# Low words of the experts' second matrices and of their token blocks, made by adding transfers in place of VectorE subtractions

## The chip, the cores and the metric

The kernel runs on one core of one Trainium2 chip. The metric is the device time of one execution in microseconds; what is compared is the median over several executions. All inputs and outputs are float32.

## The reference

Three stages follow each other: an attention with a feature map, a feed-forward layer (FFN), and a mixture of experts (MoE).

```python
def _attn_ref(q, k, v, w_phi):               # 4 batches, 8 heads, 576 tokens, 64 wide
    ...
    num = np.einsum('bhsf,bhfd->bhsd', q_p, kv)
    den = np.einsum('bhsf,bhf->bhs', q_p, z)[..., None] + 1e-06
    return (num / den).astype(np.float32)

def _moe_ref(x, U, V, w_ch1, w_ch2):         # FFN: 512 -> 2048 -> 512
    ...
    u = x + h.transpose(0, 2, 1)
    ch = np.maximum(u @ w_ch1, 0.0) @ w_ch2
    return (u + ch).astype(np.float32)

def _moe2_ref(x, w_gate, w_local, w1, w2):   # 8 experts, each 512 -> 1024 -> 512
    ...
            h = np.maximum(x[b, s] @ w1[e], 0.0)
            out[b, s] = p[e] * (h @ w2[e])
    return out.astype(np.float32)
```

## The kernel before

**Two words for each number.** TensorE multiplies float32r, a float32 with fewer bits. To keep float32 accuracy each matrix stands in two words: the high word is the value rounded to float32r, the low word what is left, rounded again. A product is three matmuls: high by high, high by low, low by high (`three`, L1168 to L1170, and `mm2`, L1494 to L1496). So a tile of weights `w` holds [high, low] of 128 x 512, and a tile of tokens `x` holds [high, low] of two 128-row blocks, 288 tokens wide in the MoE (384 in the FFN).

**Who makes the words.** `w_end` makes a weight tile: ScalarE (ACT) casts the float32 buffer to the high word (L379), then the low word is buffer minus high word, on VectorE (DVE) or GpSimd (POOL) as `either` picks; in the late part it picks VectorE (`both`, L373). `x_end` does the same for token tiles: the cast at L651, the subtraction through `paused` (L76).

```python
nc.scalar.copy(out=w[:, 0], in_=f[:, :512])
eng = yield from either(eng, 512, f, w)
both(eng, w[:, 1], f, f32(w[:, 0]), ALU.subtract)
```

**The MoE stage.** For each of the 4 batches the expert that most tokens chose is computed for the whole batch, in two units of half of its hidden width each; the other experts' tokens are handled by a loop at the end. A unit has four pieces of the first matrix, named A (seven sums of them for batches 1 to 3, where a seven-product scheme is used), and four pieces of the second matrix, named V (`VS`). The token blocks of the MoE have the key "m": 4 tiles for batch 0 and 7 for each other batch. Weights come from HBM by SyncE's (SP's) queue into `raw` and `row` buffers (L604, L608). When a low word is made, its source buffer goes back to a free list, and the next load may take it. There are 14 weight tiles, 9 token tiles and 8 `row` buffers.

**What sets the order.** The program is written out by a planner in Python, before anything runs. TensorE's order is a list of products, gone through step by step; after each step `side` lets side jobs (generators) put instructions onto the other engines. `gate` and `either` hold a job back until the planner's own clock for the engine and the buffers (`free`, `touched`) says that it would start no later than TensorE's clock plus a slack. All engines then run their instructions in that fixed order, joined by semaphores.

**The router.** `route(b)` chooses the expert of a batch, in stages that `PLANS` spreads over the steps: gate matmuls (L1551), two ACT copies of their result into a `row` buffer (L1552), transposes of it (L1558), small VectorE operations, transposes back (L1605), ACT copies into three `row` buffers (L1609), a scan, a reduction and a product on VectorE (L1612, L1616, L1619), and two small transfers on POOL's queue (L1623 `mine`, L1624 `sall`). It waits with its stages while no `row` buffer is free. POOL's queue also carries the FFN's token loads (L756).

Of the kernel before, what the change touches and what calls it, by code (L numbers as in the profile page):

```python
# [8 lines left out]
F32R = mybir.dt.float32r  # L9
# [3 lines left out]
ALU = mybir.AluOpType  # L13
# [30 lines left out]
def model(ctx, tc, kq, vx, wphi, ident, up, vp, wff, wg, wmoe1, wmoe2, rconst, outT):  # L44
    nc = tc.nc
# [12 lines left out]
    def f32(ap):  # L58
        return ap.bitcast(F32)
# [14 lines left out]
    def paused(eng, **kw):  # L74

        eng.tensor_tensor(**kw)  # L76
        if eng is nc.gpsimd and pauses[0] and free["POOL"] >= landed[0]:
            nc.gpsimd.drain()

    def in_halves(eng, dst, a, b, n, op):  # L80

        for sl in (slice(0, n // 2), slice(n // 2, n)):
            paused(eng, out=dst[:, sl], in0=a[:, sl], in1=b[:, sl], op=op)
# [82 lines left out]
    late = {}  # L166
# [3 lines left out]
    free = {"PE": 0.0, "DVE": 0.0, "ACT": 0.0, "POOL": 0.0}  # L170
    port = [0.0]
    touched = {}
# [13 lines left out]
    def cost(eng, n):  # L186
        return {"DVE": 0.085 + n / 960, "ACT": 0.17 + n / 1330, "POOL": 0.05 + n / 340}[eng]
# [4 lines left out]
    def book(eng, dur, *keys):  # L192

        at = max([free[eng]] + [touched.get(id(k), 0.0) for k in keys])
        free[eng] = at + dur
        for k in keys:
            touched[id(k)] = free[eng] + SYNC
        return free[eng]

    def gate(eng, dur, *keys):  # L200

        if not late:
            yield "step"
        while late and not force[0]:
            at = max([free[eng], port[0] if eng == "DVE" else 0.0] + [touched.get(id(k), 0.0) for k in keys])
            if at + (0.0 if eng == "POOL" else dur) <= free["PE"] + SLACK[eng][at_step[0]]:
                break
            yield "wait"
        emitted[0] += 1
        force[0] = False  # L210
        if late:
            if eng == "DVE":
                free[eng] = max(free[eng], port[0])
            at = book(eng, dur, *keys)
            if eng == "DVE":
                port[0] = at

    def either(eng, n, *keys):

        if not late:  # L220
            yield "step"
            emitted[0] += 1
            return eng
        while True:
            best = None
            for e, name, bias in ((nc.gpsimd, "POOL", 0.0), (nc.vector, "DVE", BIAS)):
                dur = cost(name, n)
                at = max([free[name], port[0]] + [touched.get(id(k), 0.0) for k in keys])
                ok = (name == "DVE" or not lean[0]) and at + (0.0 if name == "POOL" else dur) <= free["PE"] + SLACK[name][at_step[0]]
                if (ok or force[0] and (name == "DVE" or not lean[0])) and (best is None or at + dur + bias < best[0]):  # L230
                    best = (at + dur + bias, e, name, dur)
            if best is not None:
                break
            yield "wait"
        emitted[0] += 1
        force[0] = False
        free[best[2]] = max(free[best[2]], port[0])
        port[0] = book(best[2], best[3], *keys)
        return best[1]

    def transfer(kb, at=None):

        wire[0] = max(free["PE"] if at is None else at, wire[0]) + kb / 400
        return wire[0] + 2.5
# [46 lines left out]
    def later(on, issue):  # L291

        if late:
            waiting.append((touched.get(id(on), 0.0), issue))
        else:
            issue()
# [8 lines left out]
    def take(free_):  # L305

        while not free_:
            yield "blocked"
        return free_.pop(0)

    BLOCKS = ("A11", "A12", "A21", "A22")
    VS = ("V1", "V0", "V3", "V2")
# [55 lines left out]
    def both(eng, out, a, b, op):  # L368
        out, a, b = out[:, :512], a[:, :512], b[:, :512]
        if eng is nc.gpsimd:  # L370
            in_halves(eng, out, a, b, 512, op)
        else:
            eng.tensor_tensor(out=out, in0=a, in1=b, op=op)  # L373

    def w_end(u, s, f, eng, back=None):

        w = u.w[s] = yield from take(wfree)
        yield from gate("ACT", cost("ACT", 512), f, w)
        nc.scalar.copy(out=w[:, 0], in_=f[:, :512])  # L379
        eng = yield from either(eng, 512, f, w)  # L380
        both(eng, w[:, 1], f, f32(w[:, 0]), ALU.subtract)
        u.done.add(s)
        if back is not None:
            back.append(f)
# [83 lines left out]
    def w_more():  # L468
# [9 lines left out]
        def end(s, f, back=None):  # L478
            spawn("w", 2, w_end(u, s, f, nc.gpsimd, back))
# [25 lines left out]
    def w_seven(u, get, free_, eng, p, due, flat=False, pre=""):  # L505

        def end(s, f, back=None):
            spawn("w", due + (flat and s[0] == "S"), w_end(u, pre + s, f, eng, back))
# [49 lines left out]
    def w_ffn(u, due):  # L558

        def get(name):  # L560
            while (u, name) not in pieces:
                yield "blocked"
            return pieces.pop((u, name))

        spawn("w", due, fetch(u, ZSEVEN if u.g in ZU else SEVEN) if u.g > 1 else parked(u, SEVEN))
        yield from w_seven(u, get, rows, nc.gpsimd, nc.gpsimd, due)
        if u.g in ZU:
            yield from w_seven(u, lambda s: get(ZV[s]), rows, nc.gpsimd, nc.gpsimd, due, pre="z")
            return
        for s in VS:  # L570
            f = yield from get(s)
            spawn("w", due, w_end(u, s, f, nc.gpsimd, rows))
# [65 lines left out]
    def spot(key, s):  # L638
# [2 lines left out]
        w = CH if key[0] == "m" else TW  # L641
        return slice(2 * k, 2 * k + 2), slice((2 * key[1] + t) * w, (2 * key[1] + t + 1) * w)

    def x_end(key, s, r, keep, own=None, then=None):

        x = xo.setdefault(key, {})[s] = yield from take(xfree)
        wanted[1] -= then is not None and key[0] == "f"
        n_ = CH if key[0] == "m" else TW
        keys = (x,) if own is None else (x, own)
        yield from gate("ACT", cost("ACT", 2 * n_), *keys)  # L650
        nc.scalar.copy(out=x[:, 0, :, :n_], in_=r)  # L651
        for k in (slice(0, 2),) if late else (slice(0, 1), slice(1, 2)):
            use = yield from either(nc.gpsimd, n_ * (k.stop - k.start), *keys)
            paused(use, out=x[:, 1, k, :n_], in0=r[:, k], in1=f32(x[:, 0, k, :n_]), op=ALU.subtract)
        if keep:
            def send():
                nc.sync.dma_start(out=f32(xd[key[1]][XD.index(s)]), in_=f32(x))
                if late:
                    transfer(768)
            later(x, send)  # L660
        xdone.add((key, s))
        if then is not None:
            then()
# [4 lines left out]
    def x_plain(key, names):  # L668

        for s in names:  # L670
            k, t = spot(key, s)
            yield from x_end(key, s, y[:, k, t], key[0] == "p" and s != "B12")

    def x_sums(key, due):
# [18 lines left out]
        def end(s, r, then=None):  # L693
            spawn("x", due, x_end(key, s, as_x(r), True, r, (lambda: rows.append(r)) if then is None else then))
# [16 lines left out]
    def x_diff(key, due):  # L711
# [11 lines left out]
        def end(s, r, then=None):  # L723
            spawn("x", due, x_end(key, s, as_x(r)[:, :, :w], keep, r, (lambda: rows.append(r)) if then is None else then))
# [1220 lines left out]
```

## Time and profile before

| what | value |
|---|---|
| median of 3 executions | 759.97 us (759.38 to 762.55) |
| the profiled execution | 760.08 us |
| its span, first to last instruction | 758.2 us |
| PE, PEld, DVE, ACT, POOL busy | 745.3, 724.1, 637.7, 351.7, 72.5 us |
| granted TensorE clock | 1.0 |
| bytes moved by DMA | 124.27 MB |

PE is TensorE's matmuls and PEld its weight loads, which overlap them. Matmuls are pipelined, so one matmul's duration is longer than the distance to the next. Some records of matmuls can be missing. Issuing a DMA is not counted as busy on SP and ACT; the time to landing is listed apart. The trace's line numbers are those of the kernel before; in the changed kernel the same lines stand 12 or 25 further down.

### The profile page before, as it was taken

The page shows a single profiled execution, that of the slowest core. Times are in us where ns is not written, and L with a number is a line of the kernel's source. Part 1 is how long each engine was busy: PE and PEld are TensorE (multiplying, and loading weights), DVE is VectorE, ACT ScalarE, POOL GpSimd, SP SyncE. Part 2 cuts the span into 40 slices and gives each one's busy share as a digit, 9 for nine tenths or more (in the row PEclk, how much of TensorE's full clock was granted, in tenths as well). Part 3 has the DMA queues.
Part 4 walks back from the last instruction along what each step waited for, and adds up shares of the span by engine and source line. Part 5 has one row for each costly group of instructions (what it writes and reads, how often), then busy time and mean ns, then how long its engine had stood idle before and what let it go on. Part 6 is the DMA issues. An engine that isn't in the chain of part 4 may idle for free. (4 is left out here: it accounts for less than half of the span.)

```text
span 758.2 us, 18724 instructions
## 1 busy us (share of the span) xinstructions
PE 745.3 (98%) x7656; PEld 724.1 (96%) x7656; DVE 637.7 (84%) x1277; ACT 351.7 (46%) x769; POOL 72.5 (10%) x116
## 2 busy tenths in 40 slices
PE   7999999999999999999999999999999999999997
PEld 5899898999999999999999999999999999999997
DVE  6889899777569999999799485879877899999975
ACT  5677777665152343313223133343545455555450
POOL 0212233111110000100101001010000000000000
PEclk9999999999999999999999999999999999999999
DMA  6444755324468897950469004482363144243421
GB/s 203 151 132 126 260 183 189 111 80 154 181 242 328 302 332 284 346 171 29 166 241 339 18 1 157 153 287 84 114 210 101 32 125 143 68 136 108 136 69 65
DMA packets 52728, 124.27 MB, mean 164 GB/s; under 512 B 5472, under 2 KB 29152, under 8 KB 52640
## 3 DMA queue, kind: packets, MB, share of 16 engines
q1 hardware_dynamic: 43024, 87.20, 34.1%
q0 software_dynamic: 6160, 32.39, 12.3%
q10 hardware_dynamic: 3456, 3.46, 1.3%
q8 instruction: 61, 1.00, 0.5%
q14 instruction: 27, 0.22, 0.1%
HBM read 88.81 MB, written 34.23 MB: 162 GB/s over the span
## 5 line engine op out<-in xcount | busy, mean ns | idle before, releaser
L1169 PE MATMUL psf<-x,w 128*128 128x384 f32 (+1 forms) x576 | 184.1, 320 | 0.6 <-POOL x L76 0.6
L1168 PE MATMUL psf<-x,w 128*128 128x384 f32 (+1 forms) x576 | 184.4, 320 | 0.0
L1170 PE MATMUL psf<-x,w 128*128 128x384 f32 (+1 forms) x576 | 183.9, 319 | 0.0
L1494 PE MATMUL psf<-h,w 128*128 128x384 f32 (+1 forms) x576 | 182.8, 317 | 0.0
L1495 PE MATMUL psf<-h,w 128*128 128x384 f32 (+1 forms) x576 | 182.3, 316 | 0.0
L1496 PE MATMUL psf<-h,w 128*128 128x384 f32 (+1 forms) x576 | 182.2, 316 | 0.0
L1146 ACT ACTIVATE h<-psf 128x384 fp32r<-128x384 f32 (+1 forms) x144 | 62.9, 457 | 106.7 <-DVE psf L1129 77.7
L1168 PEld LDWEIGHTS psf<-x,w 128*128 128x128 f32 x576 | 108.3, 188 | 1.4 <-issue 1.4
L1169 PEld LDWEIGHTS psf<-x,w 128*128 128x128 f32 x576 | 108.2, 188 | 1.0 <-POOL x L76 0.9
L1494 PEld LDWEIGHTS psf<-h,w 128*128 128x128 f32 x576 | 108.1, 188 | 0.5 <-issue 0.5
L1170 PEld LDWEIGHTS psf<-x,w 128*128 128x128 f32 x576 | 108.2, 188 | 0.0
L1495 PEld LDWEIGHTS psf<-h,w 128*128 128x128 f32 x576 | 108.1, 188 | 0.0
L1496 PEld LDWEIGHTS psf<-h,w 128*128 128x128 f32 x576 | 108.1, 188 | 0.0
L1129 DVE TENSOR_TENSOR y<-psf,y 128x384 f32<-128x384 f32 (+1 forms) x132 | 69.1, 530 | 24.9 <-PE psf L1496 21.3
L1131 DVE SCALAR_TENSOR_TENSOR h<-psf,h 128x384 fp32r<-128x384 f32 (+1 forms) x148 | 69.0, 508 | 21.5 <-ACT h L1146 20.9
L379 ACT CAST w<-row 128x512 fp32r<-128x512 f32 x79 | 46.7, 620 | 53.9 <-DVE row L373 31.8
L373 DVE TENSOR_TENSOR w<-row,w 128x512 fp32r<-128x512 f32 x79 | 52.9, 687 | 10.6 <-ACT w L379 10.6
L857 DVE TENSOR_REDUCE mx<-pj 128x6 f32<-128x768 f32 (+2 forms) x49 | 45.8, 935 | 6.8 <-PE pj L854 6.7
L858 DVE TENSOR_TENSOR pg<-pj,mx 128x768 f32<-128x768 f32 (+2 forms) x49 | 46.1, 941 | 2.5
L887 PE MATMUL kv<-vt,ek 128*64 128x65 f32 (+1 forms) x1152 | 47.1, 230 | 0.8 <-DMA vt<-in_vx 0.8
L756 POOL DMA_DIRECT2D x<-xd x41 | 22.0, 535 | 269.4 <-PE psf L1170 232.5
L1129 DVE TENSOR_TENSOR u<-psf,p 128x384 f32<-128x384 f32 (+1 forms) x64 | 32.4, 513 | 15.3 <-PE psf L1170 14.2
(136 smaller groups left out, 1126.7 us busy)
## 6 DMA issues: line engine op xcount, KB each, us to landing
x<-xd POOLq DMA_DIRECT2D x41, 768.0 KB, 6.9
raw<-in_wff SPq DMA_DIRECT2D x32, 512.0 KB, 3.6
xd<-x SPq DMA_DIRECT2D x21, 768.0 KB, 4.9
raw<-in_wmoe SPq DMA_DIRECT2D x35, 256.0 KB, 3.4
kq<-in_kq SPq DMA_DIRECT2D x14, 576.0 KB, 4.5
row<-in_wmoe SPq DMA_DIRECT2D x29, 256.0 KB, 4.0
vt<-in_vx SPq DMA_DIRECT2D x16, 325.0 KB, 3.0
ud<-y SPq DMA_DIRECT2D x4, 1152.0 KB, 6.6
```

Source lines behind the costliest of these rows:

```text
L373: eng.tensor_tensor(out=out, in0=a, in1=b, op=op)
L379: nc.scalar.copy(out=w[:, 0], in_=f[:, :512])
L887: nc.tensor.matmul(out[c], lhsT=e[:, half, i, c], rhs=rhs, start=(tl == 0 and half == 0), stop=(tl == 8 and half == 1), skip_group_check=True)
L1129: nc.vector.tensor_tensor(**kw)
L1131: nc.vector.scalar_tensor_tensor(op1=op1, **kw)
L1146: hat[t, f] = act(lambda: nc.scalar.activation(out=hhi, in_=src, func=ACTF.Relu), n_, ready)
L1168: nc.tensor.matmul(ps, lhsT=w[:, 0, c], rhs=x[:, 0, k, :n_], start=(first and k == 0), stop=False, skip_group_check=True)
L1169: nc.tensor.matmul(ps, lhsT=w[:, 0, c], rhs=x[:, 1, k, :n_], start=False, stop=False, skip_group_check=True)
L1170: nc.tensor.matmul(ps, lhsT=w[:, 1, c], rhs=x[:, 0, k, :n_], start=False, stop=(stop and k == 1), skip_group_check=True)
L1494: nc.tensor.matmul(ps, lhsT=wh, rhs=hhi, start=(k == 0), stop=False)
L1495: nc.tensor.matmul(ps, lhsT=wl, rhs=hhi, start=False, stop=False)
L1496: nc.tensor.matmul(ps, lhsT=wh, rhs=hlo, start=False, stop=(k == 3))
```

## The change

For the V pieces of the experts' matrices (`added`) and for all token tiles of the MoE, in the late part of the program, the subtraction on VectorE or GpSimd is replaced by two steps: ACT writes the negated high word into the low word's place, and a DMA on POOL's queue adds the float32 value onto it. The source buffer is booked as busy until the larger of the planner's estimate of the transfer and `ADD_LAT`, 4.0, after the issue.

```diff
+    ADD_LAT = 4.0
+
+    def added(u, s):
+        return u.kind=="moe" and s in VS
+
     def w_end(u, s, f, eng, back=None):
 
         w = u.w[s] = yield from take(wfree)
         yield from gate("ACT", cost("ACT", 512), f, w)
         nc.scalar.copy(out=w[:, 0], in_=f[:, :512])
-        eng = yield from either(eng, 512, f, w)
-        both(eng, w[:, 1], f, f32(w[:, 0]), ALU.subtract)
+        if late and added(u, s):
+            yield from gate("ACT", cost("ACT", 512), f, w)
+            nc.scalar.mul(out=w[:, 1], in_=f32(w[:, 0]), mul=-1.0)
+            yield from gate("POOL", 0.6, f, w)
+            nc.gpsimd.dma_start(out=w[:, 1], in_=f.bitcast(F32R)[:, :512], accum_op=ALU.add)
+            touched[id(w)] = touched[id(f)] = max(transfer(512, free["POOL"]), free["POOL"] + ADD_LAT)
+        else:
+            eng = yield from either(eng, 512, f, w)
+            both(eng, w[:, 1], f, f32(w[:, 0]), ALU.subtract)
...
+    def x_low(x, r, keys, n_):
+
+        for k in (slice(0, 2),) if late else (slice(0, 1), slice(1, 2)):
+            use = yield from either(nc.gpsimd, n_ * (k.stop - k.start), *keys)
+            paused(use, out=x[:, 1, k, :n_], in0=r[:, k], in1=f32(x[:, 0, k, :n_]), op=ALU.subtract)
...
         nc.scalar.copy(out=x[:, 0, :, :n_], in_=r)
-        for k in (slice(0, 2),) if late else (slice(0, 1), slice(1, 2)):
-            use = yield from either(nc.gpsimd, n_ * (k.stop - k.start), *keys)
-            paused(use, out=x[:, 1, k, :n_], in0=r[:, k], in1=f32(x[:, 0, k, :n_]), op=ALU.subtract)
+        if late and key[0] == "m" and True:
+            yield from gate("ACT", cost("ACT", 2 * n_), *keys)
+            nc.scalar.mul(out=x[:, 1, :, :n_], in_=f32(x[:, 0, :, :n_]), mul=-1.0)
+            yield from gate("POOL", 0.6, *keys)
+            nc.gpsimd.dma_start(out=x[:, 1, :, :n_], in_=r.bitcast(F32R), accum_op=ALU.add)
+            at = max(transfer(576, free["POOL"]), free["POOL"] + ADD_LAT)
+            for k in keys:
+                touched[id(k)] = at
+        else:
+            yield from x_low(x, r, keys, n_)
```

**How the order moves.** TensorE's order differs in one place: the third router's gate matmuls. Before, they stand by themselves (`wg_sb` is the gate matrix, `psf` a PSUM bank), and 36 product rows lie between them and their transposes:

```order
L1169 MATMUL psf<-x_3706,w_3694 128x288
L1170 MATMUL psf<-x_3706,w_3694 128x288
L1551 MATMUL psf<-y,wg_sb 32x288 x8
L1168 MATMUL psf<-x_106,w_101 128x288
L1169 MATMUL psf<-x_106,w_101 128x288
```

In the changed kernel they come later on TensorE, and the transposes (`id_sb` is the identity) stand right behind them:

```order
L1194 MATMUL psf<-x_3706,w_3696 128x288
L1195 MATMUL psf<-x_3706,w_3696 128x288
L1576 MATMUL psf<-y,wg_sb 32x288 x8
L1583 MATMUL psf<-id_sb,row_86 128x128 x4
L1583 MATMUL psf<-id_sb,row_86 64x128
L1193 MATMUL psf<-x_106,w_105 128x288
```

The transposes read `row_86`, which ACT fills from the gate matmuls' banks; nothing lies between the two any more.

On ACT, in the same place, the order before has the router's copies, casts of weights (L379) and the rectified products (L1146):

```order
L1146 ACTIVATE h_95<-psf 128x288
L1552 COPY row_91<-psf 128x288 x2
L379 CAST w_3698<-raw_92 128x512
L1146 ACTIVATE h_95<-psf 128x288
L379 CAST w_103<-raw_93 128x512
L379 CAST w_98<-raw_93 128x512
L1146 ACTIVATE h_94<-psf 128x288
```

and the changed one has a negation (L387 for `w`, L672 for `x`) behind the casts of V pieces and token blocks:

```order
L1171 ACTIVATE h_94<-psf 128x288
L384 CAST w_3697<-row_85 128x512
L387 ACTIVATE w_3697<-w_3697 128x512
L1171 ACTIVATE h_96<-psf 128x288
L1577 COPY row_86<-psf 128x288 x2
L1602 ACTIVATE r_ex<-r_sh 128x40
L384 CAST w_101<-raw_92 128x512
L387 ACTIVATE w_101<-w_101 128x512
L1171 ACTIVATE h_96<-psf 128x288
```

In the whole program ACT gains 57 such negations, and VectorE loses 57 subtractions.

On POOL, before, the last token load of the FFN is followed by the routers' pairs alone:

```order
L756 DMA x_3705<-xd_113 128x1536
L1623 DMA mine_6595<-row_84 8x576
L1624 DMA sall<-row_84 8x576
L1623 DMA mine_7025<-row_88 8x576
L1624 DMA sall<-row_88 8x576
```

In the changed kernel the 57 adding transfers (L674 for `x`, L389 for `w`) stand among them, of which the first are:

```order
L781 DMA x_3705<-xd_113 128x1536
L674 DMA x_3702<-y 128x2x288
L674 DMA x_108<-y 128x2x288
L674 DMA x_106<-y 128x2x288
L674 DMA x_3706<-y 128x2x288
L1648 DMA mine_6606<-row_84 8x576
L1649 DMA sall<-row_84 8x576
L389 DMA w_3693<-row_84 128x512
L389 DMA w_104<-row_89 128x512
```

## Rows read from the trace of the kernel before

**Rows 1.** The page: the span, and the busy time of each engine.

```profile
span 758.2 us, 18724 instructions
PE 745.3 (98%) x7656; PEld 724.1 (96%) x7656; DVE 637.7 (84%) x1277; ACT 351.7 (46%) x769; POOL 72.5 (10%) x116
```

**Rows 2.** PE's waits, whole span: us in total, times, longest; largest and last late ones.

```profile
PE pj L854 <- DMA wphi_sb<-in_wphi: 3.2, 1, 3.2
...
PE psf L1169 <- POOL x L76: 0.6, 1, 0.6
...
PE psf L1168 <- DVE y L1129: 0.3, 1, 0.3
```

**Rows 3.** The same view for PEld between 530 and 758 us.

```profile
PEld psf L1168 <- issue: 0.9, 2, 0.5
PEld psf L1551 <- issue: 0.6, 3, 0.2
PEld psf L1494 <- issue: 0.5, 1, 0.5
```

**Rows 4.** Windows of the MoE: length, then busy us and (count) per engine, clock, DMA, GB/s.

```profile
core 0: us, PE busy (x) PEld busy (x) DVE busy (x) ACT busy (x) POOL busy (x), PEclk, DMA share, GB/s
560.00:600.00 40.00, 40.00 (x320) 38.27 (x319) 30.33 (x75) 23.43 (x55) 2.00 (x4) 1.00 0.31 97
...
650.00:700.00 50.00, 50.00 (x382) 50.00 (x381) 48.29 (x99) 28.18 (x60) 0.00 (x0) 1.00 0.37 115
700.00:753.50 53.50, 53.38 (x405) 53.14 (x403) 43.32 (x94) 21.01 (x48) 0.00 (x0) 1.00 0.28 90
sum 223.50, PE 223.38 PEld 220.36 DVE 193.91 ACT 112.61 POOL 4.01; mean PE 44.68 PEld 44.07 DVE 38.78 ACT 22.52 POOL 0.80
```

**Rows 5.** Groups of instructions by form, whole span: busy us, mean ns of one.

```profile
L373 DVE TENSOR_TENSOR w<-row,w 128x512 fp32r<-128x512 f32 x79 | 52.9, 687 | 10.6 <-ACT w L379 10.6
...
L379 ACT CAST w<-row 128x512 fp32r<-128x512 f32 x79 | 46.7, 620 | 53.9 <-DVE row L373 31.8 <-PE psf L1496 17.4 <-PE psf L1169 4.6
...
L756 POOL DMA_DIRECT2D x<-xd x41 | 22.0, 535 | 269.4 <-PE psf L1170 232.5 <-ACT p L1304 18.2 <-DVE h L1131 13.9
...
L76 DVE TENSOR_TENSOR x<-y,x 128x576 fp32r<-128x576 f32 x13 | 9.8, 754 | 2.3 <-ACT x L651 2.3
...
L651 ACT CAST x<-y 128x576 fp32r<-128x576 f32 x13 | 8.6, 670 | 0.0
```

**Rows 6.** DMA view, whole span: POOL's queue; issues with size, median us to landing.

```profile
q0 software_dynamic: 6160, 32.39, 12.3%
...
x<-xd POOLq DMA_DIRECT2D x41, 768.0 KB, 6.9
...
raw<-in_wmoe SPq DMA_DIRECT2D x35, 256.0 KB, 3.4
...
row<-in_wmoe SPq DMA_DIRECT2D x29, 256.0 KB, 4.0
...
mine<-row POOLq DMA_DIRECT2D x4, 18.0 KB, 1.8
```

**Rows 7.** The timeline at the third router: start us, us, what.

```profile
560.24 1.18 PE L1551 MATMUL psf<-y,wg_sb 128*32 128x288 f32 x16
...
561.05 0.89 ACT L1552 COPY row<-psf 128x288 f32<-128x288 f32 x2 [0.30 <-PE psf L1551]
...
561.34 0.40 PE L1168 MATMUL psf<-x,w 128*128 128x288 f32 x1
```

**Rows 8.** The timeline behind it, the same columns.

```profile
566.20 0.71 PE L1558 MATMUL psf<-id_sb,row 128*128 128x128 f32 x5
...
567.21 0.74 DVE L1619 TENSOR_TENSOR row<-row,row 8x576 f32<-8x576 f32 x1
```

## Prediction

> **What bounds the kernel now.** I read the page's busy times first: PE is busy for 745.3 of 758.2 us, and DVE for 637.7 [rows 1]. A pipelined PE can be called busy and still be late, so the second view is PE's own waits. The reader should see how little there is. The longest is 3.2 us at the very start, for the first load. The last ones that have to do with products come from the FFN, 0.6 us for a POOL subtraction and 0.3 us for a DVE addition [rows 2]. Between 530 and 758 us, which holds all of the MoE, PE has no wait row at all. Its weight loads have 2.0 us in three rows, all put down to "issue", that is, to no other engine [rows 3]. Third, the windows by stage: between 530 and 753.5 us PE is busy for 223.38 of 223.50 us. From 650 to 700 us it starts 382 matmuls in 50.00 us, one every 0.131 us, with the clock at 1.0, the upper of its two levels [rows 4]. In the same window DVE is busy for 48.29 of 50 us. So DVE is nearly full and is still never what PE waits for. **The stage that the change touches is bound by PE's own pace, and DVE works just below it.**
>
> **The change part by part.** My sum is made against the profiled execution: 758.2 us of span and 1.9 us around it, 760.08 us in all, 0.1 us above the median of 759.97.
>
> *Removed from DVE.* Each of 8 units has 4 V pieces, so 32 subtractions at 0.687 us go; token tiles are 4 + 3 x 7 = 25, at 0.754 us [rows 5]. That is 22.0 + 18.9 = 40.8 us of DVE's 193.9 [rows 4], leaving 153 us. What of it lies on the path that sets the end? Nothing, as PE waits for DVE nowhere in this stage [rows 2, 3]. Gain 0. Its ends are 0 and 2.0 us: if all of the weight loads' "issue" rows were DVE's lateness in disguise, 2.0 us would be back. They stand where the gate matmuls or the products after them start, which the change keeps, so I take 0.
>
> *Added to ACT.* 57 negations of the same shapes as the casts beside them, 0.620 and 0.670 us [rows 5]: 32 x 0.62 + 25 x 0.67 = 36.6 us. ACT goes from 112.6 us of 223.5 [rows 4] to 149, from 50% to 67%. An instruction behind a negation on ACT starts up to 0.67 us later; those that PE depends on are the rectified products and the copies out of PSUM. What covers this is the ring of 8 PSUM banks: a bank of six matmuls takes PE 0.79 us, so a delay of 0.67 us is less than one bank. Cost 0. If the cover fails each time, the end is 57 x 0.65 = 37 us; it is far off, because ACT keeps a third of its time and the planner puts each negation only where its clock has room.
>
> *Added to POOL and the DMA engines.* 57 issues; a POOL issue takes 0.535 us [rows 5], 30.5 us of an engine that is busy for 4 us in this stage [rows 4]. The transfers are 32 x 256 KB and 25 x 288 KB, 15.8 MB. No row shows an adding transfer, or one from SBUF to SBUF. **Time to landing:** the nearest by size are the weight loads at 3.4 and 4.0 us; on the same queue stand 18 KB at 1.8 us and 768 KB at 6.9 us, the latter in a stage with far more traffic [rows 6]. I take 4 us, near the row of the same size, with 1.8 and 6.9 us as ends. The Trainium skill (DMA: Bandwidth & Descriptors, Anatomy of one DMA) gives about 2.0 us plus bytes over 436 GB/s for such a transfer, an estimate of 2.6 us for 256 KB; for 768 KB it gives 3.8 us where the row has 6.9, so the row decides, and by either the sum stays as it is.
>
> Who waits for the landing? (a) PE, for the low word. I counted matmuls between each of the 57 issues and the first matmul that reads its low word, in the order in which the built program's instructions are written: at least 90, which at 0.131 us is 11.8 us. Even 6.9 us, plus an engine that runs a microsecond or two late, fits. (b) SP, whose next load into the source buffer waits; that load's cast follows at least 8 us later, and mostly 14 or more. (c) ACT in one place: the third router's copies back (L1609) write into two `row` buffers that transfers for token tiles read, the nearer issued 32 matmuls or 4.2 us earlier. At 4 us this just fits; at 6.9 us ACT stands for some 2.7 us, two of the intervals of 12 matmuls (1.6 us) at which PE then fills one of its 8 banks. Cost 0, and 0 to 1 us as ends.
>
> *Moved: the third router.* Its first stage waits until a `row` buffer is free, and buffers are now held longer. So gate matmuls and transposes come together on PE, with ACT's two copies between. From the rows: the gate matmuls start at 560.24, the two copies end at 561.94, and PE goes on at 561.34 [rows 7]. In the new place PE would have to wait for the copies, 0.60 us, of which two of the five transposes (0.71 us for all [rows 8]), which need the first copy alone, fill about 0.2. That is 0.4 us. There is one more condition: the buffer that the copies write is still read by the second router's product on DVE, 567.21 to 567.95 [rows 8], and the gate's new place, 12 matmuls behind the old transposes and without the gate's 1.1 us ahead of them, is about 566.5 to 567.6. If that product is as late as before, the copies end at 567.95 + 0.89 = 568.84 and PE loses 1.0 us instead. DVE has less to do, so I take 0.5; ends 0.4 and 1.0.
>
> **Sum:** 760.08 + 0.5 = 760.6, and 0.1 less against the median: **760.5 us**, no difference that can be told.
>
> **The rivals.**
>
> *Transfers in each other's way: slower.* The place is POOL's queue ahead of a unit's second products. Against it: the queue moved 32.39 MB in 12.3% of the span, 93 us or 2.9 us for a MB [rows 6]. At that rate a transfer holds the engines for 0.8 us, and for 1.7 us if the read of its target doubles it; in all 45 to 91 us more, on a DMA share of 0.28 to 0.37 [rows 4] over 223.5 us: 0.5 to 0.8. For it: nothing in the trace shows how fast the engines add. The tightest group is a token tile and four V pieces, issued within 7 us, the last one 11.8 us ahead of its use. Five of them fit into 18.9 us, so it decides from 3.8 us of engine time each. At 4.1 us, PE waits 5 x 0.3 = 1.5 us for each of 8 units: 12 us, **772.5 us**. The Trainium skill says that transfers started from different engines still share the same DMA engines and interleave (DMA: Bandwidth & Descriptors, Issuing engines are not separate DMA queues); by that rule the weight loads on SP's queue would be held up as well, and it speaks against the change. Chance 0.10.
>
> *ACT becomes the late engine: slower.* If one negation in seven stands in front of a rectification that PE already waits for, 8 x 0.65 = 5 us: **765.6 us**. For it: 67% busy, in order. Against it: the banks. Chance 0.05.
>
> *A little of the 2.0 us comes back.* DVE falls from 87% to 69% of the stage; with the third router's 0.5 us against 1.5 of the 2.0 us, **759.0 us**. Chance 0.10, inside "same".
>
> *Faster by more than can be missed.* It would need 3.8 us of PE's time where rows 3 and 4 show 2.0 us. I see no place; 0.02 for what I overlook.
>
> **How the numbers follow.** The forecast has the remaining 0.73. A measurement of this kernel tells about 0.5%, 3.8 us, from no change. Within it lie the forecast and the third rival: 0.83. Slower are the first two, 0.15; faster 0.02. The range goes from 758.0 us (all of the 2.0 us back) to 766.0 us, which takes in the late ACT; it leaves out the transfers in each other's way.
>
> **What would show it.** Right: PE's waits in the MoE hold one new entry, a transpose that waits for ACT's copy for under 1 us; DVE near 153 us and ACT near 149 us in the stage; adding transfers that land in 3 to 5 us; a DMA share of 0.5 to 0.8. Wrong: PE or its weight loads waiting for a DMA `w<-row`, `w<-raw` or `x<-y`, landings over 10 us, or rectified products that start later behind PE than before.

## The result and the profile after

| | before | after |
|---|---|---|
| median of the runs, us | 760.08 (759.38 to 762.55) | 768.18 (766.67 to 769.43) |
| ratio after : before, 95% interval | | 1.0105 [1.0094, 1.0116] |
| span of the profiled execution, us | 758.2 | 766.4 |

The change makes the kernel 8.1 us slower. The forecast was 760.5 us with a range up to 766.0, so the result lies outside the range, on the side to which 0.15 was given.

The page of the kernel after, span and busy times, answers to [rows 1]:

```profile
span 766.4 us, 18852 instructions
PE 747.4 (98%) x7656; PEld 725.7 (95%) x7656; DVE 603.9 (79%) x1220; ACT 383.7 (50%) x826; POOL 129.6 (17%) x173
```

DVE lost 57 instructions and 33.8 us, ACT gained 57 and 32.0 us, POOL's busy time grew by 57.1 us. PE makes as many matmuls as before. So the 8.2 us of span must be time in which PE stood still or ran slowly, and its waits over the whole span (us in total, times, longest) say where, against [rows 2]:

```profile
PE psf L1583 <- ACT row L1577: 4.6, 2, 3.4
...
PE psf L1193 <- DVE u L1154: 1.9, 1, 1.9
...
PE psf L1193 <- DVE y L1154: 0.3, 1, 0.3
```

L1583 are a router's transposes, L1577 are ACT's copies of its gate's product, and L1193 is a product whose PSUM bank DVE has not read yet. Two entries are new, 6.5 us in sum. The windows of the MoE, with the columns of [rows 4], give the rest:

```profile
530.00:560.00 30.00, 30.00 (x197) 28.97 (x196) 18.68 (x54) 16.18 (x34) 6.06 (x8) 1.00 0.82 190
560.00:600.00 40.00, 35.37 (x270) 33.14 (x270) 19.87 (x52) 22.26 (x52) 10.01 (x11) 0.96 0.73 172
600.00:650.00 50.00, 48.15 (x366) 47.90 (x366) 38.68 (x103) 34.67 (x74) 15.93 (x18) 1.00 0.70 161
650.00:700.00 50.00, 50.00 (x381) 50.00 (x380) 38.70 (x85) 38.48 (x81) 17.89 (x18) 1.00 1.00 226
```

From 560 to 600 us PE lacks 4.63 us and its mean clock is 0.96; from 600 to 650 it lacks 1.85 us; from 650 on it lacks nothing, although the DMA engines are busiest just there, at 1.00. A window of the same view around the first hole has the clock:

```profile
570.00:574.00 4.00, 3.56 (x17) 3.46 (x18) 2.31 (x8) 2.07 (x6) 2.00 (x4) 0.63 0.82 140
```

The timeline there (start us, us, what) shows the same from single matmuls:

```profile
570.44 0.97 PE L1583 MATMUL psf<-id_sb,row 128*128 128x128 f32 x5 [3.42 <-ACT row L1577]
...
571.92 0.44 PE L1193 MATMUL psf<-x,w 128*128 128x288 f32 x1
...
572.16 0.44 PE L1194 MATMUL psf<-x,w 128*128 128x288 f32 x1
...
572.40 0.44 PE L1195 MATMUL psf<-x,w 128*128 128x288 f32 x1
```

The matmuls start every 0.24 us where [rows 4] has one every 0.131: PE runs at the lower of its two levels, 1.2 GHz. Just before, it had stood idle for 3.42 us. Set against the same matmuls of the kernel before, those behind the hole lose another 1.5 us. Holes and slow matmuls, 6.5 + 1.5 = 8.0 us, are the loss.

**Why the copies are late.** The timeline of ACT ahead of the hole:

```profile
562.61 1.36 ACT L384 CAST w<-raw 128x512 fp32r<-128x512 f32 x2 [2.57 <-DMA raw<-in_wmoe]
...
565.14 0.62 ACT L384 CAST w<-row 128x512 fp32r<-128x512 f32 x1 [0.35 <-DMA row<-in_wmoe]
...
567.06 0.62 ACT L384 CAST w<-row 128x512 fp32r<-128x512 f32 x1 [0.99 <-DMA row<-in_wmoe]
```

ACT works in order and stands in casts whose weight loads have not landed, 3.9 us in three waits; its activations and the router's copies are queued behind them. The copies start at 570.00 us, and ACT is busy without a break from 567.06 us until then, with two of the new negations, 1.26 us, among what it does. In the kernel before the casts in this place wait for no DMA; the first one starts 4.8 us after its load was issued (at 557.03 us, below):

```profile
561.83 0.62 ACT L379 CAST w<-raw 128x512 fp32r<-128x512 f32 x1
```

The DMA view of this stretch, 545 to 575 us (KB each, median us to landing), first before, then after:

```profile
raw<-in_wmoe SPq DMA_DIRECT2D x6, 256.0 KB, 4.2
ys<-y SPq DMA_DIRECT2D x4, 384.0 KB, 2.9
row<-in_wmoe SPq DMA_DIRECT2D x3, 256.0 KB, 4.6
```

```profile
ys<-y SPq DMA_DIRECT2D x4, 384.0 KB, 6.1
...
raw<-in_wmoe SPq DMA_DIRECT2D x5, 256.0 KB, 6.5
...
row<-in_wmoe SPq DMA_DIRECT2D x3, 256.0 KB, 6.4
```

And the timeline of SP's queue, first before, then after:

```profile
557.03 1.94 SPq L604 DMA_DIRECT2D raw<-in_wmoe  x3
```

```profile
555.51 4.17 SPq L616 DMA_DIRECT2D raw<-in_wmoe  x3
```

The three loads start 1.5 us earlier than before, and SP's waits in this stretch name ACT and DVE but no transfer, so no buffer that a transfer held came free late for them. The issues themselves take 4.17 us instead of 1.94, and the loads land about 2 us later; the first of the three takes 7.1 us. What they meet is the four adding transfers of the first MoE unit, issued from 548.1 to 551.4 us, together with four stores of 384 KB: the DMA share of 550 to 560 us rose from 0.56 to 1.07 (a packet's whole time is booked where it starts, so a share can pass 1). By the Trainium skill (DMA: Bandwidth & Descriptors, Issuing engines are not separate DMA queues) transfers that different engines start share the same DMA engines; the trace agrees, since with transfers on POOL's queue the loads on SP's land in 6.5 us instead of 4.2 and the stores in 6.1 instead of 2.9.

**What an adding transfer takes.** POOL's queue over the whole span, against [rows 6], with the landings of two of the four kinds (the others: 5.4 and 6.6 us):

```profile
q0 software_dynamic: 17568, 48.16, 24.9%
...
w<-row POOLq DMA_DIRECT2D x19, 256.0 KB, 5.2
...
x<-row POOLq DMA_DIRECT2D x12, 288.0 KB, 5.5
```

24.9% of 766.4 us is 190.8 us, 12.3% of 758.2 was 93.3. The difference, 97.5 us over 57 transfers, is 1.71 us of all 16 engines for each.

### The profile page after: what moved, and what is told of

Read it like the earlier page. It is cut to its first block, busy times and chain, and to the rows that moved or that the text cites. A ratio compares the mean times of both kernels' runs of the same rounds, so it can differ in the third digit from the quotient of the medians.

```text
span 766.4 us, 18852 instructions
## 1 busy us (share of the span) xinstructions
PE 747.4 (98%) x7656; PEld 725.7 (95%) x7656; DVE 603.9 (79%) x1220; ACT 383.7 (50%) x826; POOL 129.6 (17%) x173
## 3 DMA queue, kind: packets, MB, share of 16 engines
q0 software_dynamic: 17568, 48.16, 24.9%
## 5 line engine op out<-in xcount | busy, mean ns | idle before, releaser
L1193 PE MATMUL psf<-x,w 128*128 128x384 f32 (+1 forms) x576 | 185.2, 322 | 1.9 <-DVE u L1154 1.9
L1193 PEld LDWEIGHTS psf<-x,w 128*128 128x128 f32 x576 | 109.1, 189 | 3.0 <-DVE u L1154 2.1
L373 DVE TENSOR_TENSOR w<-row,w 128x512 fp32r<-128x512 f32 x60 | 40.4, 686 | 10.4 <-ACT w L384 10.4
```

The lines of the kernel that those rows point to most:

```text
L1193: nc.tensor.matmul(ps, lhsT=w[:, 0, c], rhs=x[:, 0, k, :n_], start=(first and k == 0), stop=False, skip_group_check=True)
```

## The experiments

Theories: **D**, the adding transfers hold the DMA engines, weight loads land late, and ACT's casts stand in front of what PE needs; **A**, ACT has too much to do; **P**, the planner takes 4.0 us for a landing and so makes a wrong order; and, at first, the place of the third router alone. Diffs are against the changed kernel unless it is said otherwise.

**e1: gate and transposes one step apart.**

```diff
+            began = r[0]
             while r[0] < len(r[3]) and 16 * (i - r[2]) + step >= r[3][r[0]]:
+                if r[0] == 1 and began == 0:
+                    break
```

> The changed kernel, with the third router's transposes one step (12 matmuls, 1.6 us) behind its gate matmuls instead of right behind them. The trace of the changed kernel has three new holes on PE: 3.4 us at those transposes with 1.5 us of half-speed matmuls behind it, 1.5 us at the fourth router's, 2.0 us at a product that waits for DVE and ACT. Theory order (the collapsed stages make the first hole): about 5 us less, 763 us, ratio 1.004. Theory late ACT (ACT is already behind because its casts wait for late loads, and whatever stands behind it waits): the 1.6 us of room takes only 1.6 us off the hole, 766 us or more, ratio 1.008, and the hole stays at the transposes with 1.5 to 2 us.

Measured: 769.4 us, ratio 1.0114 [1.0097, 1.0131], no better. PE's waits:

```profile
PE psf L1583 <- ACT row L1577: 3.2, 2, 1.6
PE psf L1193 <- DVE u L1154: 1.7, 1, 1.7
PE psf L1193 <- ACT y L1537: 1.5, 1, 1.5
```

The transposes wait less, but a wait appears elsewhere, at another thing that ACT delivers, and the three rows come to 6.4 us, nearly the 6.5 of the changed kernel. The clock stays at 1.00 here, and yet the time is no shorter; 1.8 us of the profiled execution lie ahead of the first of the FFN's products (138.07 us against 136.31), so these rows do not account for all of it. That gate and transposes stand together is not the cause.

**e2: the kernel before, with the third router's gate directly ahead of its transposes.** Against the kernel before:

```diff
-    PLANS = (..., (2, 5, 7, 9, 11, 14, 16, 18, 20, 22, 25), (2, 5, 7, ...))
+    PLANS = (..., (5, 5, 7, 9, 11, 14, 16, 18, 20, 22, 25), (2, 5, 7, ...))
```

> The kernel before, with nothing changed but that the third router's gate matmuls are put right in front of their transposes, as the changed kernel has them. Theory order (that place alone is what costs): 4 to 5 us more, 764 to 765 us, ratio 1.006. Theory late ACT (the place costs only what the prediction said when ACT is on time): 0.4 to 1.0 us more, 760.5 to 761 us, ratio 1.001, and PE waits at the transposes for under 1.2 us.

Measured: 760.85 us, ratio 1.0007 [0.9997, 1.0018]. In the MoE PE waits for the copies 0.2 us:

```profile
PE psf L1558 <- ACT row L1552: 0.2, 1, 0.2
```

The place alone costs about the 0.5 us that the prediction gave it, too little to be told from nothing.

**e3: only the V pieces by transfers. e4: only the token tiles.**

```diff
-        if late and key[0] == "m" and True:
+        if late and key[0] == "m" and False:
```

```diff
-        return u.kind=="moe" and s in VS
+        return False
```

> The changed kernel with the transfers for the V pieces alone (32 of 57); the token tiles' low words are made by VectorE again. The third router's gate then stands in its old place. Theory order: both router holes and most of the third go, 760 to 761 us, ratio 1.001. Theory engine time of the transfers (each holds the 16 engines for 1.7 us, so loads are late in proportion): 32/57 of 8 us stays, 764.5 us, ratio 1.006.

> The changed kernel with the transfers for the token tiles alone (25 of 57). The third router's gate stays right in front of its transposes. Theory order: the first hole stays in full, 764 to 766 us, ratio 1.006. Theory late ACT through the V pieces' transfers: ACT is on time at the third router, the hole there is about 0.5 us, and what is left is the fourth router, whose copies wait for a token tile's transfer: 761 to 763 us, ratio 1.003.

Measured: e3 763.2 us, ratio 1.0033 [1.0021, 1.0045]; e4 763.41 us, ratio 1.0042 [1.0022, 1.0062]. Together that is 0.0075 of the 0.0105. e3 lies between its two forecasts, and e4 0.4 us above the one that it bears out. ACT's waits between 530 and 766 us in e3, and after them PE's in e4:

```profile
ACT w L384 <- DMA raw<-in_wmoe: 2.6, 1, 2.6
```

```profile
PE psf L1193 <- DVE u L1154: 1.5, 1, 1.5
```

In e3 the same load is as late as in the changed kernel, and PE waits nowhere for more than 0.6 us, as the router stands in its old place. In e4 the router is moved, ACT's casts wait for loads 0.6 us in all, and the transposes have no wait row. So in the profiled executions the hole of 3.4 us needs both: late loads from the V pieces, and a router whose copies stand behind them. Four of e4's twelve executions took 764.2 to 769.2 us at a mean clock of 0.995 to 0.997, the others had 0.999 or 1.000; slow matmuls in those four are likely, but they have no trace that shows it.

**e5: transfers that copy instead of adding.**

```diff
-            nc.gpsimd.dma_start(out=w[:, 1], in_=f.bitcast(F32R)[:, :512], accum_op=ALU.add)
+            nc.gpsimd.dma_start(out=w[:, 1], in_=f.bitcast(F32R)[:, :512])
...
-            nc.gpsimd.dma_start(out=x[:, 1, :, :n_], in_=r.bitcast(F32R), accum_op=ALU.add)
+            nc.gpsimd.dma_start(out=x[:, 1, :, :n_], in_=r.bitcast(F32R))
```

> The 57 transfers write their source over the negated high word instead of adding to it; the low words are then the whole value (this part of the computation is changed), and every instruction stands where it stood in the changed kernel. Theory D (the DMA engines are held by the transfers, so weight loads land late and ACT's casts, in order, wait in front of the router's copies): an adding transfer took 97.5/57 = 1.71 us of the 16 engines; if the read of the target is half of it, a copy takes about 0.85, the queue's extra time falls from 97 to about 49 us, the weight loads land in 3.5 to 4 us, the transposes' wait falls from 3.4 to under 1 us: 761 to 764 us. Theory A (ACT has 36.6 us more to do, and that is what makes the copies late): ACT's work is the same, 767 to 769 us. Theory P (the planner takes 4.0 us for a landing that takes 5 to 6.6): landings of about 4 us would fit its estimate, 760 to 762 us.

Measured: 761.4 us, ratio 1.0015 [1.0005, 1.0026]. With every instruction in its place, 6.8 of the 8.1 us come back. POOL's queue and the weight loads of 545 to 575 us:

```profile
q0 software_dynamic: 17568, 48.16, 19.2%
```

```profile
raw<-in_wmoe SPq DMA_DIRECT2D x5, 256.0 KB, 4.3
...
row<-in_wmoe SPq DMA_DIRECT2D x3, 256.0 KB, 4.7
```

19.2% of 759.9 us less the 93.3 is 52.6 us, 0.92 us for a copy against 1.71 for an addition. The loads land as in the kernel before, the first cast starts at 560.24 us without a wait, and PE's wait for the router's copies is gone. This result is what theory D gave. Against A it speaks plainly: ACT's work is the same. It does not tell what the two negations ahead of the copies add once ACT is late. Theory P gave this time too; e7 decides it.

**e6: the kernel before with the 57 negations, no transfers.** Against the kernel before; DVE's subtractions write over what ACT made:

```diff
+        if late and u.kind == "moe" and s in VS:
+            yield from gate("ACT", cost("ACT", 512), f, w)
+            nc.scalar.mul(out=w[:, 1], in_=f32(w[:, 0]), mul=-1.0)
         eng = yield from either(eng, 512, f, w)
...
+        if late and key[0] == "m":
+            yield from gate("ACT", cost("ACT", 2 * n_), *keys)
+            nc.scalar.mul(out=x[:, 1, :, :n_], in_=f32(x[:, 0, :, :n_]), mul=-1.0)
```

> The kernel before, with the 57 negations on ACT put in front of DVE's subtractions, which write over them: ACT has the changed kernel's load, DVE its old one, and there are no adding transfers. Theory D: no transfer is late, 760 to 761.5 us, PE's waits in the MoE under 1 us. Theory A: ACT comes late without any transfer, PE waits for ACT 3 to 5 us in sum, 763 to 768 us. Theory P: as D.

Measured: 762.53 us, ratio 1.0033 [1.0019, 1.0048], between the two forecasts. PE's longest waits in the MoE are short:

```profile
PE psf L1501 <- DVE w L373: 0.9, 1, 0.9
PE psf L1176 <- DVE w L373: 0.4, 2, 0.2
PE psf L1174 <- DVE u L1135: 0.4, 1, 0.4
```

Two of the three rows are products that wait for a subtraction, which here stands behind its negation; the changed kernel has no such wait. The planner also drew the fourth router's gate to its transposes, which costs little: from the products ahead of both to those behind both, PE loses 0.3 us against the kernel before. So with loads in time ACT's added work and these waits together cost some 2.5 us. ACT's part alone is not measured here; e5, with the same work on ACT, bounds it at 1.1 us by its ratio, and e10 tests it for one unit.

**e7: the planner told longer landings.**

```diff
-    ADD_LAT = 4.0
+    ADD_LAT = 6.5
...
-                touched[id(t)] = max(transfer(256), touched.get(id(t), 0.0) + 3.2)
+                touched[id(t)] = max(transfer(256), touched.get(id(t), 0.0) + 5.3)
...
-            touched[id(r)] = max(transfer(384), touched.get(id(r), 0.0) + 3.5)
+            touched[id(r)] = max(transfer(384), touched.get(id(r), 0.0) + 6.0)
```

> The changed kernel, its planner told longer landings: 6.5 instead of 4.0 us for an adding transfer, 5.3 instead of 3.2 for a weight load, 6.0 instead of 3.5 for a row load. PE's order stays as it was, and ACT and DVE change only in which of two buffers a piece uses. Theory P (a wrong estimate sets the order): 760 to 763 us. Theory D: the estimate moves little, 766 to 769 us.

Measured: 768.21 us, ratio 1.0115 [1.0098, 1.0132]; the longest wait of the transposes is again 3.4 us. Theory P falls.

**e8: the gate's copies on DVE.**

```diff
-            nc.scalar.copy(out=gl[:, c * CH:(c + 1) * CH], in_=ps)
+            (nc.vector.tensor_copy if b >= 2 else nc.scalar.copy)(out=gl[:, c * CH:(c + 1) * CH], in_=ps)
```

> The changed kernel with the third and fourth router's copies of the gate's product (L1577) on DVE instead of ACT, nothing else moved. Theory D, by which the 3.4 us hole and the slow clock behind it come from ACT's queue standing in casts of late loads ahead of these copies: the wait of the transposes falls to 0.5 to 1.5 us, the clock stays up, 762.5 to 765 us; the hole of 2 us before 623 stays. If the copies are late for another reason (their buffer, the gate's own matmuls, or DVE stands behind late loads just as ACT does), the wait stays at 2 us or more and the time at 766 to 769 us.

Measured: 768.99 us, ratio 1.012 [1.0103, 1.0137]: theory D's first forecast missed, and the second, 766 to 769 us, holds. PE's wait, and the timeline of DVE ahead of the third router's copies:

```profile
PE psf L1583 <- DVE row L1577: 6.6, 2, 4.7
```

```profile
565.08 0.46 DVE L1156 SCALAR_TENSOR_TENSOR h<-psf,h 128x288 fp32r<-128x288 f32 x1 [3.02 <-ACT h L1171]
...
569.45 0.46 DVE L1156 SCALAR_TENSOR_TENSOR h<-psf,h 128x288 fp32r<-128x288 f32 x1 [1.70 <-ACT h L1171]
...
571.46 0.80 DVE L1577 COPY row<-psf 128x288 f32<-128x288 f32 x2
```

DVE has time (79% busy), but its queue is in order too, and ahead of the copies it stands twice, 4.7 us in sum, in operations that need ACT's activations, which stand behind the late casts. Moving the copies changes which queue holds them, not what it waits for.

**e9: the first MoE unit's four V pieces back on DVE. e10: the same, but ACT still makes the four negations.**

```diff
-        return u.kind=="moe" and s in VS
+        return u.kind=="moe" and s in VS and (u.b, u.g) != (0, 0)
```

```diff
+            if (u.b, u.g) == (0, 0):
+                eng = yield from either(eng, 512, f, w)
+                both(eng, w[:, 1], f, f32(w[:, 0]), ALU.subtract)
+            else:
...
```

> The changed kernel, but for the four V pieces of the first MoE unit, whose low words DVE subtracts again: 4 of 57 transfers and 4 negations go, PE's order stays. These are the four issued between 548 and 552 us, beside four 384 KB stores and ahead of the next weight loads. Theory D, local form: that collision makes the load that ACT's cast waits for at 562.6 us land in 7.1 us; without the four, the loads behind them land in about 4 us, the 3.4 us wait of the transposes goes under 1 us and the half-speed matmuls behind it go too: 762.5 to 765 us, and the hole of 2 us before 623 may stay. If the loss is spread over all transfers, four of 57 give back 0.6 us: 767 to 768 us.

> As the run before, but ACT still makes the four negations, and DVE's subtractions write over them: only the four transfers go. Theory D: the same time as the run before, within 0.5 us, 762.5 to 765 us. Theory A (ACT's negations make its copies late): as the changed kernel, 767 to 769 us.

Measured: e9 763.62 us, ratio 1.006 [1.0039, 1.0081]; e10 763.58 us, ratio 1.0044 [1.003, 1.0058]. The third router's transposes in e9 and in e10 on PE's timeline, and the window in e10 in which the changed kernel had its slow matmuls:

```profile
567.71 1.03 PE L1583 MATMUL psf<-id_sb,row 128*128 128x128 f32 x5
```

```profile
567.20 0.85 PE L1587 MATMUL psf<-id_sb,row 128*128 128x128 f32 x5 [0.59 <-ACT row L1581]
```

```profile
570.00:574.00 4.00, 4.00 (x33) 4.00 (x32) 3.25 (x10) 3.15 (x7) 1.68 (x2) 1.00 0.67 115
```

Four of 57 transfers carry some 4.6 of the 8.1 us by the medians (3.4 and 4.6 by the ratios), and it is the transfers: with their negations kept the time is the same. The hole of 3.4 us is gone in e9 and is 0.6 us in e10, and the clock of both profiled executions stays at 1.00 there. What is left of PE's wait for copies is the fourth router's, 0.8 us in e9 (at 595.09 us) and 0.65 in e10. Two of e9's five executions took 765.5 and 766.9 us, and no trace shows why.

**e11: only the last two batches' 30 transfers. e12: only the first two batches' 27.** For e11 (e12 has `< 2` in both places):

```diff
-        return u.kind=="moe" and s in VS
+        return u.kind=="moe" and s in VS and u.b > 1
...
-        if late and key[0] == "m" and True:
+        if late and key[0] == "m" and key[1] > 1:
```

> Only the 30 transfers of the last two batches' units stay (16 V pieces, 14 token tiles); the first 27 low words are DVE's again. PE's order is that of the kernel before. Theory D, by which a transfer costs only where a tight chain (a load, its cast on ACT, a copy or activation behind it) has no slack: no router and no 384 KB store stands beside these 30, so 760 to 761.5 us, ratio under 1.002. If each transfer costs its share, 30/57 of 8.1 us is 4.3 us: 764.4 us.

> The other half: only the 27 transfers of the first two batches' units stay, with the third router where the change has it. Theory D: nearly all of the loss, 766 to 768.5 us, with the transposes' wait at 3 to 4 us. If each transfer costs its share, 27/57 of 8.1 us is 3.8 us: 763.9 us.

Measured: e11 760.6 us, ratio 1.0001 [0.9992, 1.001]; e12 769.6 us, ratio 1.0117 [1.0101, 1.0132]. In e11 the third router stands in its old place. PE's only wait after 500 us is this row, and the window with most of its transfers is full of matmuls:

```profile
PE psf L1193 <- DVE y L1154: 0.3, 1, 0.3
```

```profile
650.00:700.00 50.00, 50.00 (x382) 50.00 (x381) 38.60 (x83) 37.02 (x75) 15.09 (x15) 1.00 0.90 203
```

Thirty transfers cost nothing, with the DMA engines busy for 0.90 of these 50 us; twenty-seven cost all. In e12 the transposes' longest wait is again 3.4 us; the time is 1.1 us above its forecast, and its profiled execution, the slowest of four, has half-speed matmuls behind a second hole as well. So a transfer has no fixed price here. It costs where something in a queue ahead of PE's next input is due before the delayed load.

No run beats the kernel before. e11 equals it with 30 instructions and 17.7 us less on DVE, for which PE does not wait.

## Why the prediction was wrong

- **Nothing to gain from DVE: right.** PE did not wait for it before, and e11 takes 30 of its instructions away at no change. The amount was 33.8 us instead of 40.8.
- **ACT at no cost: right for what was tested.** In e10 four negations change nothing, and e5, with all 57, is 1.1 us above the kernel before in all, by its ratio. What negations cost behind late casts, where two of them stood ahead of the router's copies, was not tested. The rows of the negations in the changed kernel have 632 and 685 ns, close to the 620 and 670 taken.
- **Landing in 4 us, ends 1.8 and 6.9: size off, and beyond the upper end where it mattered.** The medians are 5.2 to 6.6 us. The token tiles' transfers (L674) have this spread, and over 10 us was among the prediction's signs of being wrong:

```profile
DMA to landing us min/median/max: 3.9/5.7/10.4
```

  The Trainium skill (DMA: Bandwidth & Descriptors, Anatomy of one DMA) gives an estimate of 2.6 us for 256 KB, which is further off; the measurement decides. A POOL issue took 0.535 us in the rows of before and 0.85 to 1.30 in those of after, again without anybody who waited.
- **(a) PE and the low words: right.** No product waits for a transfer; PE has no wait row for a DMA in the MoE.
- **(b) "SP, whose next load into the source buffer waits; that load's cast follows at least 8 us later": this step failed.** I looked only for those who wait for the *buffers* of a transfer. The loads that came late had their buffers in time and were even issued earlier. They share the *engines*: landing went from 4.2 to 6.5 us, the lead of a cast over its load was 4.8 us in the kernel before (557.03 to 561.83 us), and so the cast waited. What the prediction put at nothing here cost PE the hole of 3.4 us and 1.5 us of slow matmuls; e9 and e10, without the four transfers of this place, give some 4.6 us of it back. A lead that is measured in the old kernel holds the old landing time; a change that lengthens all landings has to be set against every lead, not only against its own.
- **(c) The third router's tile copies and the transfer: right place, mis-sized.** I gave ACT a wait of 0 to 2.7 us and PE a cost of 0 to 1. ACT waited 4.6 us:

```profile
ACT row L1634 <- DMA x<-row: 4.6, 1, 4.6
```

  The transfer that it waited for was issued at 581.61 us and landed 9.5 us later, where the prediction allowed 6.9. PE's price is the second, 1.2 us entry of the transposes' 4.6 us row, the fourth router's:

```profile
599.59 0.85 PE L1583 MATMUL psf<-id_sb,row 128*128 128x128 f32 x5 [1.21 <-ACT row L1577]
```

  The runs show that the two go together: this wait of ACT and the fourth router's hole are 3.5 and 0 us in e5, 3.7 and 0.3 in e7, 4.0 and 0.6 in e12, 4.2 and 0.8 in e9, 4.6 and 1.2 in the changed kernel. By these rows ACT has room for an estimated 3.4 us.
- **The third router's move at 0.5 us: right by itself (e2), wrong beside the rest.** The term took ACT's two copies to come as promptly as in [rows 7]. They stood behind late casts, 3.4 us, and the slow matmuls followed.
- **The rival "transfers in each other's way": the right resource, the wrong place.** It had 1.7 us of engine time as its upper value, as measured, and a DMA share of 0.8, where 0.70 to 1.00 came between 530 and 700 us. It then asked only from what point PE would wait for low words, found that safe, and got 0.10. That weight loads on SP's queue are held up as well, 6.5 us instead of 4.2, was the mechanism; it should have been priced by the leads of the casts. The prediction had it only as a rule of the Trainium skill (DMA: Bandwidth & Descriptors, Issuing engines are not separate DMA queues), with which the trace agrees.
- **The rival "ACT becomes the late engine" named the symptom, 765.6 us.** ACT was late, but from waiting: its 383.7 us are 50% of the span.

What stays open: of the 8.0 us that PE lost, the 1.9 us in which it waits for a DVE result. Such a wait, of 1.2 to 1.5 us, remains in e4, e5, e9 and e10, and is 0.4 in e3 and absent in e11. In the changed kernel ACT has stores and a cast, which wait for DVE, ahead of the PSUM copies that DVE then needs, and before it had them behind. That this order is its cause was not tried.

## What to carry to other kernels

The transfers on POOL's queue were paid for by the loads on SP's: when a kernel gets new transfers, list the leads of all loads in that stretch, from issue to first use, and compare them with a longer landing, before looking at the buffers of the new transfer. The price lies in a few places: spare the stretch in which stores, loads and an in-order engine's casts already meet, and the same transfers can be free elsewhere. When a late input stands at the head of an in-order queue, moving the work behind it to another engine does not help if that engine waits for the first one.

## What the hardware showed that was not expected

- An adding transfer of 256 or 288 KB from SBUF to SBUF took 1.71 us of the 16 DMA engines, the same transfer as a copy 0.92, a ratio of 1.85. Worked out in the same way it was 1.70 us in e11 and in e12, 1.58 us for 256 KB alone (e3) and 1.91 us for 288 KB alone (e4). POOL's busy time was 129.6 us with additions and 107.1 with copies, for the same instructions: 0.39 us more for each issue.
- Issuing got slower with the load on the engines: three of SP's issues took 4.17 us instead of 1.94, and 1.67 us in e5 with the same instructions and copies in place of additions.
- After PE's idle time of 3.42 us the granted clock was 0.63 in the mean of 4 us, and matmuls came at 0.24 us. Slow matmuls also followed PE's idle times of 2.36 us in e12 (at 625.21 us) and 1.96 us in e8 (at 601.78 us), while after 1.85 us in the changed kernel (at 623.38 us) and 0.8 us in e9 it stayed at 1.00. With the 1.5 us behind it, the hole of 3.42 us cost nearly half as much again as its length.
